# First stage of a long-convolution kernel: 128-row loads of x and v, and a transposed pos_emb in place of transposes on TensorE

## The chip, the cores and the metric

The kernel runs on one core of a Trainium2 chip. The core has TensorE (PE in the profile; its weight loads are PEld), VectorE (DVE), ScalarE (ACT), GpSimd (POOL) and SyncE (SP, which here only issues DMAs), an on-chip memory of 128 partitions (SBUF), an accumulation memory for TensorE (PSUM), and 16 DMA engines that move data between SBUF and the device's DRAM. The metric is the device time of one execution in microseconds. Arrangement of the inputs on the host, before the launch, is not part of it.

## The reference

The inputs x and v are 4 x 12800 x 128 (batch, sequence, channels), pos_emb is 12800 x 64. A filter is made by a small MLP from pos_emb, the product x*v is convolved with it along the sequence, the result is gated with x, and a short gated convolution with two dense layers follows. All is float32; the three weights of the last part come in as float64.

```
h_mlp = np.maximum(pos_emb @ w1, 0.0) @ w2
h_filt = h_mlp * np.exp(-0.01 * pos)[:, None]
u = x * v
y = irfft(rfft(u, n=2 * S) * rfft(h_filt, n=2 * S), n=2 * S)[:, :S]
z = x * y
...
gate_pre[t] += conv_w[k] * z[t + k - 4]      # k = 0..4
out = (sigmoid(gate_pre) * (z @ w_val)) @ w_out
```

## The kernel before

The sequence of 12800 is seen as J x N1 x N2 = 2 x 100 x 64, and the transform is done in two steps, over the 100 and over the 64. The program has three stages, one after the other, with DRAM buffers between them.

**Stage 1** (pools `p1` and `ps1`) is the one that the change touches. Its main loop, `for n in range(N2)`, makes 64 turns, one for each value of the n2 index (`n_seq` pairs n2 with its mirror). A turn does this:

- `fetch` (L323) issues the load of the x and v rows of a later turn, seven ahead, into one of five buffers `ld` (`held`, `XB = 5`). A buffer is 128 partitions x 2048 floats: 1024 of x and 1024 of v. The rows are two batch halves x 50 folded n1 values = 100 rows of 8 KB; they lie in partitions 14 to 113 (`P0 = 14`, `PT = 114`), so that the first half ends, and the second begins, at partition 64.
- `product` (L328) multiplies x by v on VectorE, `mirrored` (L334), once for two turns, makes sum and difference of a pair on VectorE, and GpSimd subtracts one half from the other (L342).
- `spectra` (L346) multiplies by the table `fold`, 12 matmuls of 64 x 512 into two PSUM tiles `fp`; ScalarE copies each into a tile `st` (four of them).
- `store` (L359) writes the 100 rows of `st`, also partitions 14 to 113, to the DRAM buffer `a_u`.

The loads, the stores and the pos_emb loads are issued by SyncE in the order of the code, through a helper `_Split` (L112) that cuts a transfer of 100 rows into one of 96 and one of 4. The scheduler's order is taken from the code (`tc.manual_schedule`). A DMA completes on one of eight semaphores that all DMAs of SyncE and ScalarE take in turn, and an issue waits until the semaphore's previous DMA, eight earlier, has landed.

Between these turns the generator `filt` (L249) computes the filter's first transform in portions. Its parts in order are: 16 steps on pos_emb (TensorE transposes four 100 x 128 blocks into `tp`, VectorE copies `tp` to `posT`, TensorE multiplies by `w1bd` into `gp`, VectorE applies the maximum and the window and writes `g_sb`), then 32 steps `ap` (matmuls with `fwd`, copied by ScalarE to `ag`), then 25 steps on `fk` (tables built by ScalarE and VectorE, then matmuls and a ScalarE copy). Each portion yields a weight, and turn n runs portions until their sum reaches `n_fil * (n + 1) / 58` (L395): the same weight in every turn, about 1.86 of 107.9.

At the start, GpSimd clears partitions 0 to 13 of the five `ld` buffers (L368), VectorE partitions 96 to 127 of two `eo` tiles (L371), and ScalarE issues the loads of 14 constants before its first copy.

**Stage 2** reads `a_u` back in tiles of 128 partitions (`load_pair`, L219), multiplies the spectra and transforms back; **stage 3** makes the last transform, the gates and the output. Neither is changed. Stage 2 cannot begin before the last store of stage 1 has landed.

Of the kernel before, what the change touches and what calls it, by code (L numbers as in the profile page):

```python
# [9 lines left out]
F32 = mybir.dt.float32  # L10
# [3 lines left out]
ALU = mybir.AluOpType  # L14
# [9 lines left out]
B, S, D, FO, KC = 4, 12800, 128, 64, 5  # L24
J, N1, N2 = 2, 100, 64
M = N1 * N2
KG = 8
NF, NH = N1 // 2, 64
P0 = NH - NF
PT = P0 + N1  # L30
R = 4
WARM = 4
NC1 = N1 // 2 + 1
# [2 lines left out]
def _tables():  # L36
    n1, n2 = np.arange(N1), np.arange(N2)
    k1, k2 = np.arange(N1), np.arange(N2)
    th = 2 * np.pi * (np.outer(n1, 4 * k1 + 1) % (4 * N1)) / (4 * N1)
    fwd = np.stack([np.cos(th), np.sin(th), -np.cos(th)], 1)  # L40

    off = 2 * np.pi * (np.outer(2 * n1[:NF] + 1, 4 * k1 + 1) % (8 * N1)) / (8 * N1)
    fold = np.zeros((128, 3, 128))
    for r in (P0, NH):
        fold[r:r + NF, 0, P0:P0 + N1] = np.cos(off) + np.sin(off)
        fold[r:r + NF, 1, P0:P0 + N1] = np.cos(off) - np.sin(off)
    fold[:, 2] = 2 * fold[:, 0].astype(np.float32)

    inv = np.zeros((N1, 2, N2))
    inv[:, 0, :NC1] = (np.cos(th.T) + np.sin(th.T))[:, :NC1] / (2 * M)  # L50
    inv[:, 1, :NC1] = (np.cos(th.T) - np.sin(th.T))[:, :NC1] / (2 * M)
    ph = (np.outer(4 * k1 + 1, n2)[:, :, None] + 4 * N1 * np.outer(n2, k2)[None]) % (4 * M)
    ph = 2 * np.pi * ph / (4 * M)
    wr, wi = np.cos(ph), np.sin(ph)
    f = np.concatenate([np.concatenate([wr, wi], 2), np.concatenate([-wi, wr], 2)], 1)
    g = np.transpose(f, (0, 2, 1))

    ph = (2 * n2[:N2 // 2] + 1 - N2)[:, None] * (4 * N1 * k2 + (4 * k1 + 1)[:, None])[:, None] % (8 * M)
    ph = 2 * np.pi * ph / (8 * M)
    f = np.stack([np.cos(ph), np.sin(ph), -np.cos(ph), np.sin(ph)], 1).reshape(N1, 2, 2, N2 // 2, N2)  # L60
    f = f.transpose(0, 1, 3, 2, 4).reshape(N1 // 2, 2, 2 * N2, N2)
    g = np.concatenate([g[:, :, :N2] + g[:, :, N2:], g[:, :, :N2] - g[:, :, N2:]], 2)


    f = f.transpose(2, 0, 1, 3).reshape(2 * N2, N1 // 2, 1, 2 * N2)
    g = g.reshape(N1 // 2, 2, 2, N2, 2 * N2).transpose(1, 3, 0, 2, 4).reshape(2 * N2, N1 // 2, 2, 2 * N2)
    w = np.concatenate([f, g], 2)
    be = 2 * np.pi * (np.outer(2 * n2 + N2 - 1, k2) % (2 * N2)) / (2 * N2) + np.pi / 4
    cb, sb = np.sqrt(0.5) * np.cos(be), np.sqrt(0.5) * np.sin(be)
    dft = np.stack([np.block([[cb, sb], [-sb, cb]]), np.block([[-sb, cb], [-cb, -sb]])], 1)  # L70
    al = 2 * np.pi * np.outer(2 * n2 - 1, 4 * k1 + 1) / (8 * M)
    tw = np.tile(np.stack([np.cos(al), np.sin(al)], 1), (2, 1, 1))
    win = np.exp(-0.01 * np.arange(S, dtype=np.float32)).reshape(J, N1, N2)
    win = np.transpose(win, (1, 0, 2))
    tabs = {"fwd": fwd, "fold": fold, "inv": inv, "w": w, "dft": dft, "tw": tw, "win": win, "ident": np.eye(128)}
    return {k: np.ascontiguousarray(a, dtype=np.float32) for k, a in tabs.items()}
# [47 lines left out]
def tile_longconv_gate(  # L124
# [107 lines left out]
        return a2, weights[-1][:, p % PG]  # L232

    with tc.tile_pool(name="p1", bufs=1) as p1, tc.tile_pool(name="ps1", bufs=1, space=PSUM) as ps1:
        pos_v = pos.rearrange("(j a n) f -> j a n f", j=J, a=N1)

        g_sb = p1.tile([N1, J, FO, N2], F32, name="g_sb")

        HC, GN, E, XB = 8, 8, 4, 5
        held = [load() for _ in range(XB + 1)]  # L240
        pos_held = held.pop().rearrange("p (i e) -> p i e", i=2)

        def load_pos(c0):
            pos_sb = pos_held[:N1, c0 // HC % 2].rearrange("a (j n f) -> a j n f", j=J, f=FO)
            for j in range(J):
                sync_s.dma_start(out=pos_sb[:, j], in_=pos_v[j][:, c0:c0 + HC])
            return pos_sb

        def filt():  # L249

            parts, pos_sb, after = [], load_pos(0), None
            for c0 in range(0, N2, HC):
                nxt = load_pos(c0 + HC) if c0 + HC < N2 else None
                for j in range(J):
                    for n in range(0, HC, GN):
                        if after:
                            after()
                        tp = ps1.tile([128, 4, N1], F32, name="tp", bufs=1)
                        for q in range(4):
                            nc.tensor.transpose(  # L260
                                out=tp[:, q], in_=pos_sb[:, j, n + 2 * q:n + 2 * q + 2].rearrange("a n f -> a (n f)"),
                                identity=ident[:N1, :N1])
                        posT = p1.tile([128, 4, N1], F32, name="posT", bufs=2)
                        nc.vector.tensor_copy(out=posT, in_=tp)

                        def after(j=j, n0=c0 + n, posT=posT):
                            gp = ps1.tile([N1, GN, FO], F32, name="gp", bufs=1)
                            for q in range(4):
                                nc.tensor.matmul(  # L269
                                    out=gp[:, 2 * q:2 * q + 2].rearrange("a n e -> a (n e)"),  # L270
                                    lhsT=posT[:, q], rhs=w1bd, start=True, stop=True)
                            nc.vector.scalar_tensor_tensor(
                                g_sb[:, j, :, n0:n0 + GN], gp.rearrange("a n e -> a e n"), 0.0,
                                win[:, j, n0:n0 + GN].unsqueeze(1).to_broadcast([N1, FO, GN]),
                                op0=ALU.max, op1=ALU.mult)
                        yield 1.3
                pos_sb = nxt
            after()
            yield 0.7

            for j in range(J):
                for e0 in range(0, FO, E):
# [13 lines left out]
            for k0 in range(0, N1, 4):  # L296
# [9 lines left out]
                    after()  # L306

                def after(k0=k0, fk=fk):
                    gz = ps1.tile([128, 4, 2 * N2], F32, name="gp", bufs=1)
                    for i in range(4):  # L310
                        nc.tensor.matmul(
                            out=gz[:, i], lhsT=ag[:, k0 + i].rearrange("p j e -> p (j e)"), rhs=fk[:, i],
                            start=True, stop=True)
                    nc.scalar.copy(out=ag[:, k0:k0 + 4].rearrange("p k j e -> p k (j e)"), in_=gz)
# [7 lines left out]

        def fetch(i):  # L323
            t = held[i % XB]
            sync_s.dma_start(out=t[P0:PT], in_=xv[n_seq[i]].rearrange("h q w j l b d -> (h q) (w j l b d)"))
            fetched[i] = t.rearrange("p (w e) -> p w e", w=2)

        def product(i):  # L328
            t = fetched.pop(i)
            u = p1.tile([128, J * 2 * XE], F32, name="u", bufs=1) if i % 2 == 0 else t[:, 0]  # L330
            nc.vector.tensor_tensor(u[:PT], t[:PT, 0], t[:PT, 1], op=ALU.mult)
            us[i] = u

        def mirrored(q):  # L334

            a, b = us.pop(2 * q), us.pop(2 * q + 1)
            eo = held_e[q % 2]
            eng = nc.vector if q == N2 // 2 - 1 else nc.gpsimd
            for s, op in ((0, ALU.add), (1, ALU.subtract)):
                nc.vector.tensor_tensor(  # L340
                    eo[:PT, s].rearrange("p j l e -> p (j l e)"), a[:PT], b[:PT], op=op)
                eng.tensor_tensor(  # L342
                    eo[:PT, s, :, 0], eo[:PT, s, :, 0], eo[:PT, s, :, 1], op=ALU.subtract)
            eos[q] = eo

        def spectra(q, s):  # L346
# [13 lines left out]
        def store(q, s, st):  # L360
            sync_s.dma_start(
                out=a_u[:, s, q].rearrange("k e j b d -> k (e j b d)"),
                in_=st[P0:PT].rearrange("k e j b d -> k (e j b d)"))

        fetched, us, eos, last = {}, {}, {}, None
        with tc.manual_schedule():
            for t in held:
                nc.gpsimd.memset(t[0:P0], 0.0)  # L368
            held_e = [p1.tile([128, 2, J, 2, XE], F32, name=f"eo{i}") for i in range(2)]
            for t in held_e:  # L370
                nc.vector.memset(t[96:128], 0.0)  # L371
            fetch(0)
            raw_val, raw_out = _raw(nc, p1, w_val, "raw_val"), _raw(nc, p1, w_out, "raw_out")
            raw_cw = _raw(nc, p1, conv_w.rearrange("k d -> d k"), "raw_cw")
            fil = filt()
            n_fil, spent = 16 * 1.3 + 0.7 + 16 * 0.9 + 16 * 1.5 + 25 * 1.9 + 0.5, 0.0
            for i in range(1, XB):
                fetch(i)
            product(0)
            product(1)  # L380
            mirrored(0)
# [364 lines left out]
                        fill_halo(j, g // EG)  # L746


_INS = ["pos_emb", "w1", "w2", "moe_w_val", "moe_conv_w", "moe_w_out"]

_OUTS = [((J, D, N2, B, N1), "float32")]
_ORDER = np.concatenate([np.arange(NC1), np.arange(N1 - 1, NC1 - 1, -1)])
# [36 lines left out]
```

## Time and profile before

| what | us |
|---|---|
| median of three runs | 1186.93 |
| lowest and highest | 1176.95, 1187.07 |
| the profiled execution's own time | 1178.38 |
| its span, first to last instruction | 1176.2 |
| first matmul of stage 2 in it | 374.6 |

The profile is of one execution. A row of a window view gives a stretch of the span, then for each engine its busy time and instruction count, then the granted TensorE clock, the mean busy share of the 16 DMA engines and the bytes per time that they moved. A row of the chain of waits gives a start, a duration and what the end of the program was waiting for then. A row of a group gives the line, the engine, the operation, its tiles and shapes, the count, the busy time and the mean duration, and then the engine's idle time before these instructions and what ended it.

### The profile page before, as it was taken

To read this page: it belongs to the slowest core of one execution; us is meant where nothing else is said; L and a number is where in the kernel's file an instruction comes from. 1 tells how busy PE (TensorE), PEld (TensorE's weight loads), DVE (VectorE), ACT (ScalarE), POOL (GpSimd) and SP (SyncE) were. 2 spreads that over 40 slices of the span, in tenths; PEclk is the share of its full clock that TensorE was granted. 3 is DMA by queue.
4 is the path that set the end of the run, shared out by engine and by line. 5 is a ranking of instruction groups with operands and counts; after the bars stand their busy time and mean duration, and the time that the engine had idled before them with its cause. 6 is when DMAs were issued, how large, how long until landed. Compare 5 with 4: busy or idle time off the path is not lost.

```text
span 1176.2 us, 17865 instructions
## 1 busy us (share of the span) xinstructions
PE 1052.8 (90%) x6272; PEld 497.3 (42%) x6272; DVE 988.8 (84%) x1168; ACT 617.9 (53%) x1000; POOL 780.4 (66%) x398
## 2 busy tenths in 40 slices
PE   1698999788883999999999999978999999999986
PEld 0355565444431344444444444433444444444432
DVE  4376864798971899999999999818999999999996
ACT  0234766666652243444444443336676767676764
POOL 5123433233320888889988888828889898898880
PEclk9798999999996799999999999989999999999999
DMA  9799999999997688888888999567999999999932
GB/s 216 216 298 350 367 332 312 315 311 312 310 298 265 234 302 302 309 298 302 299 302 293 360 337 327 191 190 217 279 286 282 271 289 278 282 287 279 291 119 111
DMA packets 90968, 329.92 MB, mean 280 GB/s; under 512 B 10094, under 2 KB 17690, under 8 KB 77482
## 3 DMA queue, kind: packets, MB, share of 16 engines
q1 hardware_dynamic: 56904, 249.06, 68.8%
q10 hardware_dynamic: 33978, 79.74, 17.8%
q8 instruction: 51, 0.84, 0.3%
q14 instruction: 35, 0.29, 0.1%
HBM read 197.69 MB, written 131.07 MB: 280 GB/s over the span
## 4 chain that ended last, share of the span: by engine, by line
PE 64%; DMA 22%; ACT 5%; DVE 5%; issue 2%; ACTq 0%; SPq 0%; DVEq 0%
PE c_ps L459 21%; DMA a_u<-st 17%; PE z_ps L443 9%; PE sd L620 9%; PE o_ps L681 6%; PE fp L355 6%; PE v_ps L671 5%; PE tp L634 4%; PE c_ps L428 2%; DVE gt L662 2%; PE ap L289 1%; ACT gt L659 1%; PE gp L269 1%; DMA c_y<-c_sb 1%; ACT o_sb L689 1%
## 5 line engine op out<-in xcount | busy, mean ns | idle before, releaser
L647 POOL TENSOR_TENSOR ext<-yr,xr 128x400 f32<-128x400 f32 x120 | 302.9, 2526 | 41.2 <-DVE yr L645 39.1
L342 POOL TENSOR_TENSOR eo<-eo 114x512 f32<-114x512 f32 x62 | 112.1, 1822 | 219.9 <-DVE eo L340 219.9
L662 DVE SCALAR_TENSOR_TENSOR gt<-ext,cw,gt 128x1600 f32<-128x1600 f32 x128 | 240.7, 1880 | 0.8 <-ACT gt L659 0.8
L355 PE MATMUL fp<-eo,fold 64*128 64x512 f32 x768 | 193.8, 640 | 40.6 <-ACT st L357 23.1
L466 ACT COPY c_sb<-c_ps 128x1024 f32<-128x1024 f32 x100 | 101.3, 1013 | 204.6 <-PE c_ps L459 197.9
L357 ACT COPY st<-fp 128x1024 f32<-128x1024 f32 x128 | 125.2, 1014 | 125.7 <-PE fp L355 63.1
L459 PE MATMUL c_ps<-va,ld 64*128 64x512 f32 (+1 forms) x800 | 166.6, 556 | 0.2 <-ACT c_sb L466 0.2
L449 DVE TENSOR_TENSOR va<-z_ps,h_sb 128x2048 f32<-128x2048 f32 x50 | 114.3, 2285 | 38.2 <-PE z_ps L443 38.2
L528 POOL TENSOR_TENSOR va<-va,vb 128x1024 f32<-128x1024 f32 x50 | 118.4, 2367 | 40.0 <-DVE vb L449 40.0
L443 PE MATMUL z_ps<-ld 64*64 64x512 f32 x800 | 122.5, 621 | 17.6 <-DMA ld<-a_u 15.7
L681 PE MATMUL o_ps<-gd,wout 128*128 128x400 f32 x256 | 112.4, 521 | 19.7 <-DVE gd L676 10.9
L620 PE MATMUL sd<-ag,inv 100*64 100x512 f32 x512 | 128.3, 618 | 1.0 <-ACT sd_sb L627 1.0
L355 PEld LDWEIGHTS fp<-eo,fold 64*128 64x128 f32 x768 | 73.6, 197 | 120.2 <-issue 67.6
L459 PEld LDWEIGHTS c_ps<-va,ld 64*128 64x128 f32 x800 | 74.2, 189 | 113.7 <-issue 110.2
L530 POOL TENSOR_TENSOR va<-va,vb 128x1024 f32<-128x1024 f32 x50 | 118.2, 2363 | 0.0
L627 ACT COPY sd_sb<-sd 128x512 f32<-128x512 f32 x128 | 76.1, 595 | 77.0 <-PE sd L620 54.6
L449 DVE TENSOR_TENSOR vb<-z_ps,h_sb 128x2048 f32<-128x2048 f32 x50 | 114.0, 2279 | 0.0
L671 PE MATMUL v_ps<-ext,wval 128*128 128x400 f32 x256 | 107.1, 500 | 0.0
L340 DVE TENSOR_TENSOR eo<-u,ld 114x1024 f32<-114x1024 f32 x64 | 82.0, 1311 | 20.3 <-PE fp L355 17.5
L459 PE MATMUL c_ps<-vc,ld 64*128 64x512 f32 x400 | 94.2, 589 | 0.0
L634 PEld LDWEIGHTS tp<-ident,sd_sb 128*128 128x128 f32 x512 | 59.4, 143 | 78.9 <-PE sd L620 47.9
L529 POOL TENSOR_TENSOR vc<-vc,vd 128x768 f32<-128x768 f32 x50 | 91.1, 1822 | 1.9
(89 smaller groups left out, 1503.1 us busy)
## 6 DMA issues: line engine op xcount, KB each, us to landing
c_y<-c_sb ACTq DMA_DIRECT2D x100, 512.0 KB
ld<-a_u SPq DMA_DIRECT2D x49, 1024.0 KB
ld<-in_xv_dram SPq DMA_DIRECT2D x64, 768.0 KB
a_u<-st SPq DMA_DIRECT2D x64, 768.0 KB
ag<-c_y SPq DMA_DIRECT2D x116, 384.0 KB
out_dram<-o_sb ACTq DMA_DIRECT2D x32, 800.0 KB
xr<-in_xt_dram SPq DMA_DIRECT2D x31, 800.0 KB
ld<-in_tab_w_dram SPq DMA_DIRECT2D x12, 768.0 KB
```

The costliest lines, as they stand in the source:

```text
L355: nc.tensor.matmul(out=fp[:, h], lhsT=fold[r, w], rhs=eo[r, o, :, l], start=i == 0, stop=i == len(terms) - 1)
L357: nc.scalar.copy(out=st[:, o].rearrange("k j (h b) d -> k h j (b d)", h=2), in_=fp)
L443: nc.tensor.matmul(out=zs[c][half[h]], lhsT=wk[half[c], 0, half[h]], rhs=a2[half[c], h, j], start=True, stop=True)
L449: nc.vector.tensor_tensor(out, z.rearrange("p (b d) -> p b d", d=D).unsqueeze(1).to_broadcast([128, n, B, D]), h_sb.unsqueeze(2).to_broadc ...
L459: nc.tensor.matmul(out=c_ps[:, h, 0:n], lhsT=wk[half[h], 1 + c], rhs=vt[half[h]].rearrange("p b d -> p (b d)"), start=(i == 0), stop=(i == ...
L528: nc.gpsimd.tensor_tensor(va[:, 0:2], va[:, 0:2], vb[:, 0:2], op=ALU.add)
L530: nc.gpsimd.tensor_tensor(va[:, 2:4], va[:, 2:4], vb[:, 2:4], op=ALU.add)
L620: nc.tensor.matmul(out=sd[c * N2:(c + 1) * N2], lhsT=inv[:, c], rhs=ct[c][:, r * B * D:(r + 1) * B * D], start=True, stop=True)
L647: nc.gpsimd.tensor_tensor(e[:, r0 + r], yr, xr, op=ALU.mult)
L662: nc.vector.scalar_tensor_tensor(gt, rows(t, k), cw[:, k:k + 1], gt, op0=ALU.mult, op1=ALU.add)
L671: nc.tensor.matmul(out=v_ps, lhsT=wval, rhs=rows(t)[:, r * ROW:(r + 1) * ROW], start=True, stop=True)
L681: nc.tensor.matmul(out=o_ps, lhsT=wout, rhs=gd, start=True, stop=True)
```

## The change

1. **x and v.** The host appends 14 rows of zeros to each batch half, so `xv` has 128 rows per n2. `fetch` loads all of them with one DMA of 128 x 8 KB (1 MiB, before 800 KB in two DMAs). The rows now begin at partitions 0 and 64. The clears L368 and L371 are gone, and products and differences run over 128 partitions in place of 114.
2. **The table `fold`** has its rows and its result columns moved to begin at 0, so the result's rows lie in partitions 0 to 99 of `st`, and the store reads those. It is still split in 96 and 4.
3. **pos_emb.** The host lays it out as 16 blocks of 128 x 400, transposed. `load_pos` loads one block with one DMA straight into a form that the matmul takes. The transposes, `tp`, `posT` and the copies are gone, and `gp` has two buffers. Five blocks have room; four are loaded between the first loads of x and v, and each of the 16 steps issues one later load at its end.
4. **Weights.** A pos_emb step now counts 1.0 (before 1.3, and 0.7 for the last), so `n_fil` falls from 107.9 to 102.4.

```diff
-    for r in (P0, NH):
-        fold[r:r + NF, 0, P0:P0 + N1] = np.cos(off) + np.sin(off)
+    for r in (0, NH):
+        fold[r:r + NF, 0, :N1] = np.cos(off) + np.sin(off)
...
-        pos_held = held.pop().rearrange("p (i e) -> p i e", i=2)
...
+        PE1 = GN // 2 * N1
+        pos_held = held.pop()[:, 0:2048 // PE1 * PE1].rearrange("p (i q a) -> p i q a", q=GN // 2, a=N1)
+        parts, pos_ts = [(c0, j) for c0 in range(0, N2, GN) for j in range(J)], []
+
+        def load_pos():
+            if len(pos_ts) < len(parts):
+                c0, j = parts[len(pos_ts)]
+                t = pos_held[:, len(pos_ts) % (2048 // PE1)]
+                nc.sync.dma_start(out=t.rearrange("p q a -> p (q a)"), in_=pos[j, c0 // GN])
+                pos_ts.append(t)
...
-                        for q in range(4):
-                            nc.tensor.transpose(
-                                out=tp[:, q], in_=pos_sb[:, j, n + 2 * q:n + 2 * q + 2].rearrange("a n f -> a (n f)"),
-                                identity=ident[:N1, :N1])
-                        posT = p1.tile([128, 4, N1], F32, name="posT", bufs=2)
-                        nc.vector.tensor_copy(out=posT, in_=tp)
...
+            for i, (n0, j) in enumerate(parts):
+                gp = ps1.tile([N1, GN, FO], F32, name="gp", bufs=2)
+                for q in range(GN // 2):
+                    nc.tensor.matmul(
+                        out=gp[:, 2 * q:2 * q + 2].rearrange("a n e -> a (n e)"),
+                        lhsT=pos_ts[i][:, q], rhs=w1bd, start=True, stop=True)
...
+                load_pos()
+                yield 1.0
...
-            sync_s.dma_start(out=t[P0:PT], in_=xv[n_seq[i]].rearrange("h q w j l b d -> (h q) (w j l b d)"))
+            nc.sync.dma_start(out=t, in_=xv[n_seq[i]].rearrange("h q w j l b d -> (h q) (w j l b d)"))
...
-                in_=st[P0:PT].rearrange("k e j b d -> k (e j b d)"))
+                in_=st[:N1].rearrange("k e j b d -> k (e j b d)"))
...
-            for t in held:
-                nc.gpsimd.memset(t[0:P0], 0.0)
...
-            for t in held_e:
-                nc.vector.memset(t[96:128], 0.0)
...
             for i in range(1, XB):
                 fetch(i)
+                load_pos()
...
+    xv = np.stack(pairs, 3)
+    xv = np.concatenate([xv, np.zeros_like(xv[:, :, :NH - NF])], 2)
+    pos = np.asarray(inputs["pos_emb"]).reshape(J, N1, N2 // KG, KG // 2, 2, FO)
+    pos = np.transpose(pos, (0, 2, 4, 5, 3, 1)).reshape(J, N2 // KG, 2 * FO, KG // 2 * N1)
```

SyncE's queue after the first loads, before the change (`ld_102` to `ld_106` are the five x and v buffers, `ld_107` holds pos_emb, and each row is one DMA with its partitions x elements):

```order
L120 DMA ld_104<-in_xv_dram 96x2048
L120 DMA ld_104<-in_xv_dram 4x2048
L120 DMA ld_107<-in_pos_emb_dram 96x512
L120 DMA ld_107<-in_pos_emb_dram 4x512
...
L120 DMA ld_105<-in_xv_dram 96x2048
L120 DMA ld_105<-in_xv_dram 4x2048
...
L120 DMA a_u_60<-st_155 96x2048
L120 DMA a_u_60<-st_155 4x2048
```

The same queue from its first row, with the change:

```order
L306 DMA ld_102<-in_xv_dram 128x2048
L306 DMA ld_103<-in_xv_dram 128x2048
L245 DMA ld_107<-in_pos_dram 128x400
L306 DMA ld_104<-in_xv_dram 128x2048
...
L245 DMA ld_107<-in_pos_dram 128x400 x2
L306 DMA ld_105<-in_xv_dram 128x2048
L245 DMA ld_107<-in_pos_dram 128x400 x2
L118 DMA a_u_60<-st_144 96x2048
L118 DMA a_u_60<-st_144 4x2048
```

The first pos_emb load was the 17th DMA of this queue, behind eight x and v loads; it is now the third, behind two. A turn without pos_emb issues three DMAs here where it issued four.

TensorE's order from the first turn on, before (`fp` is the spectrum of x*v, `tp` the transpose, `gp` the pos_emb product):

```order
L355 MATMUL fp_156<-eo0_115,fold_63 128x512 x4
L355 MATMUL fp_162<-eo0_115,fold_63 128x512 x2
L260 MATMUL tp_174<-ident_68,ld_107 128x100 x4
L269 MATMUL gp_181<-w1bd_69,posT_179 100x128 x4
L260 MATMUL tp_187<-ident_68,ld_107 128x100 x4
L355 MATMUL fp_199<-eo0_115,fold_63 128x512 x2
L355 MATMUL fp_203<-eo0_115,fold_63 128x512 x4
```

And with the change:

```order
L334 MATMUL fp_145<-eo0_110,fold_63 128x512 x4
L334 MATMUL fp_151<-eo0_110,fold_63 128x512 x2
L252 MATMUL gp_155<-w1bd_69,ld_107 100x128 x4
L252 MATMUL gp_162<-w1bd_69,ld_107 100x128 x4
L334 MATMUL fp_173<-eo0_110,fold_63 128x512 x2
L334 MATMUL fp_177<-eo0_110,fold_63 128x512 x4
```

A `gp` matmul stood behind a transpose and VectorE's copy of it; it now reads the loaded tile itself, and two steps stand in a row between the first two turns.

More of the change, by code (lines that the diff above doesn't have):

```diff
@@ L28 @@
 NF, NH = N1 // 2, 64
-P0 = NH - NF
-PT = P0 + N1
 R = 4
@@ L43, in _tables @@
     fold = np.zeros((128, 3, 128))
-    for r in (P0, NH):
-        fold[r:r + NF, 0, P0:P0 + N1] = np.cos(off) + np.sin(off)
-        fold[r:r + NF, 1, P0:P0 + N1] = np.cos(off) - np.sin(off)
+    for r in (0, NH):
+        fold[r:r + NF, 0, :N1] = np.cos(off) + np.sin(off)
+        fold[r:r + NF, 1, :N1] = np.cos(off) - np.sin(off)
     fold[:, 2] = 2 * fold[:, 0].astype(np.float32)
@@ L234, in tile_longconv_gate @@
     with tc.tile_pool(name="p1", bufs=1) as p1, tc.tile_pool(name="ps1", bufs=1, space=PSUM) as ps1:
-        pos_v = pos.rearrange("(j a n) f -> j a n f", j=J, a=N1)
         g_sb = p1.tile([N1, J, FO, N2], F32, name="g_sb")
-        HC, GN, E, XB = 8, 8, 4, 5
+        GN, E, XB = 8, 4, 5
         held = [load() for _ in range(XB + 1)]
-        pos_held = held.pop().rearrange("p (i e) -> p i e", i=2)
[L243 to L247, printed above, removed]
@@ L249, in filt @@
-        def filt():
[L251 to L258, printed above, removed]
-                        for q in range(4):
-                            nc.tensor.transpose(
-                                out=tp[:, q], in_=pos_sb[:, j, n + 2 * q:n + 2 * q + 2].rearrange("a n f -> a (n f)"),
-                                identity=ident[:N1, :N1])
-                        posT = p1.tile([128, 4, N1], F32, name="posT", bufs=2)
[L264 to L279, printed above, removed]
@@ new lines, in filt @@
+        def filt():
+            for i, (n0, j) in enumerate(parts):
[4 more added lines that the diff above has]
+                        lhsT=pos_ts[i][:, q], rhs=w1bd, start=True, stop=True)
+                nc.vector.scalar_tensor_tensor(
+                    g_sb[:, j, :, n0:n0 + GN], gp.rearrange("a n e -> a e n"), 0.0,
+                    win[:, j, n0:n0 + GN].unsqueeze(1).to_broadcast([N1, FO, GN]),
+                    op0=ALU.max, op1=ALU.mult)
+                load_pos()
+                yield 1.0
@@ L308, in after @@
                 def after(k0=k0, fk=fk):
-                    gz = ps1.tile([128, 4, 2 * N2], F32, name="gp", bufs=1)
+                    gz = ps1.tile([128, 4, 2 * N2], F32, name="gp", bufs=2)
                     for i in range(4):
@@ L330, in product @@
             u = p1.tile([128, J * 2 * XE], F32, name="u", bufs=1) if i % 2 == 0 else t[:, 0]
-            nc.vector.tensor_tensor(u[:PT], t[:PT, 0], t[:PT, 1], op=ALU.mult)
+            nc.vector.tensor_tensor(u, t[:, 0], t[:, 1], op=ALU.mult)
             us[i] = u
@@ L339, in mirrored @@
             for s, op in ((0, ALU.add), (1, ALU.subtract)):
[L340 to L343, printed above, removed]
+                nc.vector.tensor_tensor(eo[:, s].rearrange("p j l e -> p (j l e)"), a, b, op=op)
+                eng.tensor_tensor(eo[:, s, :, 0], eo[:, s, :, 0], eo[:, s, :, 1], op=ALU.subtract)
             eos[q] = eo
@@ L375, in tile_longconv_gate @@
             fil = filt()
-            n_fil, spent = 16 * 1.3 + 0.7 + 16 * 0.9 + 16 * 1.5 + 25 * 1.9 + 0.5, 0.0
+            n_fil, spent = 16 * 1.0 + 16 * 0.9 + 16 * 1.5 + 25 * 1.9 + 0.5, 0.0
             for i in range(1, XB):
                 fetch(i)
+                load_pos()
             product(0)
@@ L746, in tile_longconv_gate @@
                         fill_halo(j, g // EG)
-_INS = ["pos_emb", "w1", "w2", "moe_w_val", "moe_conv_w", "moe_w_out"]
+_INS = ["w1", "w2", "moe_w_val", "moe_conv_w", "moe_w_out"]
 _OUTS = [((J, D, N2, B, N1), "float32")]
@@ L771 @@
         pairs.append(np.transpose(a, (5, 0, 4, 2, 3, 1, 6)))
-    feeds[:0] = [("xv", np.stack(pairs, 3)), ("xt", xt)]
+    xv = np.stack(pairs, 3)
+    xv = np.concatenate([xv, np.zeros_like(xv[:, :, :NH - NF])], 2)
+    pos = np.asarray(inputs["pos_emb"]).reshape(J, N1, N2 // KG, KG // 2, 2, FO)
+    pos = np.transpose(pos, (0, 2, 4, 5, 3, 1)).reshape(J, N2 // KG, 2 * FO, KG // 2 * N1)
+    feeds[:0] = [("xv", xv), ("xt", xt), ("pos", pos)]
     for name, a in feeds:
```

## The prediction

> **What bounds the kernel now.** I read the slices of the page first, to find the stage's limit; then the chain of waits; then windows, to price transfers of different shape; then groups and timeline, for what leaves.
>
> ```profile
> span 1176.2 us, 17865 instructions
> PE   1698999788883999999999999978999999999986
> DMA  9799999999997688888888999567999999999932
> GB/s 216 216 298 350 367 332 312 315 311 312 310 298 265 234 302 302 309 298 302 299 302 293 360 337 327 191 190 217 279 286 282 271 289 278 282 287 279 291 119 111
> ```
>
> A slice is 29.4 us. Over the first twelve, which are stage 1, the DMA engines are the full resource (9), TensorE mostly is not (8). And full is not the same as fast: the first two slices are full at 216 GB/s, the fifth at 367. The chain of waits says the same in order of time:
>
> ```profile
> 7.93 9.16 DMA w1bd<-in_w_dram
> 17.12 8.89 DMA ident<-in_tab_ident_dram
> 26.03 9.13 DMA raw_out<-in_moe_w_out_dram
> 35.18 3.83 DMA ld<-in_pos_emb_dram
> 39.01 0.91 PE tp L260 x4
> ...
> 87.11 8.32 DMA ld<-in_pos_emb_dram
> ...
> 159.85 10.61 DMA a_u<-st
> 170.52 10.50 DMA a_u<-st
> ...
> 371.90 2.60 DMA ld<-a_u
> ...
> 374.63 2.11 PE z_ps L443 x8
> ```
>
> To 39 us the chain is loads that wait for loads; from 160 us on it is one store after another, a step of 10.6 us for two turns; stage 2 starts at 374.6. So stage 1 ends when the DMA engines have done their work. What that work costs depends on the shape of the transfer:
>
> ```profile
> 0.00:372.00 372.00, 285.46 (x1960) 156.30 (x1960) 249.35 (x305) 193.17 (x286) 121.04 (x71) 0.93 0.94 299
> 30.00:60.00 30.00, 18.90 (x97) 11.75 (x98) 10.99 (x14) 9.06 (x9) 3.33 (x2) 0.72 0.79 216
> 8.00:30.00 22.00, 5.49 (x12) 1.86 (x12) 9.71 (x8) 0.00 (x0) 9.27 (x5) 0.92 1.00 224
> 120.00:160.00 40.00, 40.00 (x432) 23.65 (x428) 30.08 (x19) 29.99 (x34) 15.86 (x9) 1.00 1.00 359
> 160.00:330.00 170.00, 144.53 (x948) 78.09 (x946) 135.47 (x201) 113.27 (x198) 56.52 (x33) 0.98 0.97 313
> 340.00:344.00 4.00, 3.50 (x10) 1.57 (x12) 2.61 (x3) 1.64 (x3) 1.42 (x1) 0.57 0.99 328
> 376.00:386.00 10.00, 8.40 (x60) 3.35 (x56) 9.18 (x6) 1.14 (x3) 4.55 (x3) 0.67 1.03 406
> ```
>
> The last two numbers of a row are DMA share and GB/s. At 8 to 30 us there are x and v loads of 100 rows and small constants, no store: full at 224. At 376 to 386 us, in stage 2, there are loads of 128 partitions alone: full at 406. At 340 to 344 there are stores of 100 rows alone: 328. The mixtures lie between, 359 and 313. What was in flight shows in the issues of these stretches:
>
> ```profile
> 331.48 0.69 SPq L120 DMA_DIRECT2D ld<-in_xv_dram  x2
> 333.36 16.46 SPq L120 DMA_DIRECT2D a_u<-st  x12
> ld<-in_xv_dram SPq DMA_DIRECT2D x64, 768.0 KB
> ld<-in_xv_dram SPq DMA_DIRECT2D x64, 32.0 KB
> ld<-a_u SPq DMA_DIRECT2D x2, 1024.0 KB
> ```
>
> The last x and v load was issued at 331.5, then only stores. The third and fourth rows are all of stage 1's x and v loads, the last is what the stretch 376 to 386 moved.
>
> **The change, part by part.** The sum is DMA time against the profiled execution: 1178.38 us for a span of 1176.2, so 2.2 lie outside; it is 8.6 below the median of the runs shown and near their lowest.
>
> *DMA work before.* Share 0.94 of 372 us is 350 busy, 22 idle. The loads are 64 x 800 KB = 52.4 MB and the stores as much; pos_emb is 3.3 MB; 299 GB/s x 372 us is 111.2 MB in all, so 3.0 MB are constants and stage 2's first tiles. For the stores I have two ends: 328 GB/s (alone) and 400 (as well as 128 partitions); I take 350, near the one that was measured on stores and below the 359 of the full mixture: 52.4/0.35 = 150 us. pos_emb ran where the rate was 216 to 350, about 12 us; the 3.0 MB at 216, about 14. The loads are left with 350 - 150 - 12 - 14 = 174 us, 301 GB/s: above their rate alone, below the mixture, as it must be.
>
> *Loads of 128 rows.* 64 x 1 MiB = 67.1 MB, 14.7 MB more. The rate lies between 224 (nothing gained) and 406 (the 128-partition row). I take 400, since the row nearest in shape, 1 MiB into 128 partitions, has it: 168 us, 6 less than before. So 28% more bytes cost about nothing, if the rate holds. Break-even for this term alone is 67.1/0.174 = 386 GB/s, close by; this is the term on which the sign hangs.
>
> *Stores.* Same bytes; the rows move from partitions 14-113 to 0-99. No row shows that; ends: 400 GB/s (131 us) and 224 (234 us). I take 150, unchanged.
>
> *pos_emb.* The same 3.3 MB, in 16 DMAs for 32; with 128 rows at 350 to 400 it is 9 us, 3 less. Rest 14. Sum 168 + 150 + 9 + 14 = 341, 9 less than before.
>
> *Idle DMA time.* The stretch 30 to 60 us loses 0.21 x 30 = 6.3 us, because SyncE's pos_emb issues stood behind eight loads and behind semaphores that ScalarE's constants held, and then TensorE's order stood behind pos_emb:
>
> ```profile
> 17.48 5.49 PE L355 MATMUL fp<-eo,fold 64*128 64x512 f32 x12 [17.48 <-POOL eo L342]
> 39.01 0.90 PE L260 MATMUL tp<-ident,ld 100*128 100x100 f32 x4 [16.03 <-DMA ld<-in_pos_emb_dram]
> 30.25 0.39 ACTq L81 DMA_DIRECT2D raw_cw<-in_moe_conv_w_dram  x1
> 31.97 1.93 ACT L357 COPY st<-fp 128x1024 f32<-128x1024 f32 x2
> 43.19 4.64 PE L355 MATMUL fp<-eo,fold 64*128 64x512 f32 x12
> ```
>
> Turn 0's matmuls begin at 17.5, turn 1's at 43.2. With pos_emb third in the queue the 16.0 us wait goes. Late next is ScalarE, which cannot copy before its last constant is issued at 30.25; the third generation of each semaphore comes sooner if 128-row loads are faster, so I put turn 1 at about 25. I count 5 of the 6.3 us; the second pos_emb wait (8.3 us at 87) costs the DMA engines nothing, since they were full there. The other idle time, at the start and in the last 40 us, where stage 2's tiles wait for stores, stays: 22 - 5 = 17.
>
> *Sum.* Stage 1 ends at 341 + 17 = 358 in place of 372: -14, and to the same tail **1178.4 - 14 = 1164 us**.
>
> *What lies beside other work.* These leave the engines and are costed at nothing, or nearly:
>
> ```profile
> L260 PE MATMUL tp<-ident,ld 100*128 100x100 f32 x64 | 9.3, 273 | 18.3 <-DMA ld<-in_pos_emb_dram 18.3
> L264 DVE COPY posT<-tp 128x400 f32<-128x400 f32 x16 | 9.1, 566 | 18.0 <-PE tp L260 18.0
> 0.74 8.76 POOL L368 MEMSET ld<- 14x2048 f32 x5 [0.29 <-POOLq L762]
> L371 DVE MEMSET eo<- 32x2048 f32 x2 | 3.5, 1765 | 0.9 <-issue 0.9
> ```
>
> TensorE loses 9.3 of 285 us and VectorE 12.6 of 249, in a stage of 358: not the limit, though at 120 to 160 us TensorE is busy all 40 us, so no turn there gets shorter. The clears lie under the first loads; GpSimd's end at 9.5 us, well before the matmul at 17.5 that follows its first subtraction. Operations over 128 partitions in place of 114 take the time of their row length, which stays; bounds 0 and 128/114, 12%, of VectorE's 249, which would still be under 358. The portions' smaller weight gives each turn 1.77 in place of 1.86 of filter work, within the same 64 turns.
>
> *The added wait.* From the fifth on, a pos_emb load waits for TensorE's step that frees its slot, and behind it in SyncE's queue stand the next store and the next x and v load. Four to five loads are ahead of use, about 25 us at 5 us a turn, and the step is in the turn that TensorE is at; so 0, and at most one turn, 5 us, once. SyncE's other wait gets looser: three issues a turn on eight semaphores, not four, let 2.7 turns be in flight where 2 were.
>
> **Rivals.**
>
> *A. As summed:* 1164, with 1152 to 1174 for its own bounds (stores at 380 or at 328 GB/s, with the new loads at 400: -12 and +10).
>
> *B. Stores get faster too.* If the slow 100-row loads were what delayed the stores between them, these go from 350 to 400 GB/s: 131 us, -19 more, 1145. For it: 359 GB/s at 120 to 160 us, with the same transfers. Against it: 328 with stores alone.
>
> *C. A ceiling on the mixture.* No slice of this stage passes 367. At 359 for everything, 119.5 + 3.3 + 3.0 MB take 350 us, and with 17 idle stage 1 ends at 367: 1173, no change that can be told. Against it: 406 at 376 to 386 us, loads alone. [...]
>
> *D. Stores get slower (the other side).* That 100 rows load at 224 and 128 partitions at 406 says that the spread over partitions matters, by more than 100/128. The stored rows lay 50 below partition 64 and 50 above; now 64 and 36. If the fuller half sets the pace, a store takes 64/50 of 150, 192 us: +42 - 14, 1206. It decides from about 164 us on (320 GB/s for the stores). Against it: the half was not yet shown to be what counts, and a turn has room between stores. [...]
>
> *E. Loads gain nothing.* If they are slow for another reason and stay at 301 GB/s, 67.1 MB take 223 us, +49 for -6: 1219. Against it: the 406 row.
>
> **How the numbers follow.** About 1% (12 us) is what a measurement can tell from no change. Chances: A 0.50, B 0.15, C 0.14, D 0.13, E 0.08. The likeliest is A, 1164. The range 1140 to 1192 holds A, B and C and the beginning of D; D's and E's ends, 2 in 10, are left out. Faster by over 1% (below 1166.6) are B and somewhat over two thirds of A, and a little of C: 0.53. Same: the rest of A, most of C, a little of D: 0.29. Slower: most of D, and E: 0.18.
>
> **What would show it.** Loads right: early stretches without stores at 350 to 400 GB/s. Start right: turn 1's matmuls near 25 us, no wait for pos_emb. Stores: a stretch of stores alone at 328 to 350, and steps of about 10 us for two turns in the chain; at 12, D. End: stage 2's first matmul near 360. The forecast is wrong if the loads stay under 350 GB/s, if stores fall under 320, or if TensorE, not DMA, carries the chain from 160 us on.

## The result, and the profile after

| | before | after |
|---|---|---|
| median | 1181.94 us | 1164.05 us |
| lowest and highest, four runs each | 1173.24, 1187.07 | 1161.68, 1167.67 |
| the profiled execution's own time | 1178.38 | 1167.67 |
| its first matmul of stage 2 | 374.6 | 362.5 |

The ratio of after to before is 0.9853, with a 95% interval of 0.9818 to 0.9888: 1.5% faster, 18 us by the medians. The profiled execution of after is the slowest of its four, so the two traces differ by 10.7 us only. Three executions of before beside the experiments (1258.5, 1741.4 and 2095.7 us) ran far slower than all others and are left out here. In the traces stage 1 ends 12.1 us earlier; what follows it takes 803.0 us, before 801.6.

The span and the slices of the changed kernel's page, each slice 29.1 us:

```profile
span 1165.5 us, 17562 instructions
PE   4899887887764999999999999979999999999986
DMA  9999999999987588988888998558999999999932
GB/s 364 350 417 403 361 352 345 353 341 350 344 268 286 209 311 300 317 300 302 303 312 287 362 339 321 178 176 218 283 288 285 264 292 278 278 289 284 284 119 113
```

The first two slices, 216 GB/s before, are 364 and 350 now, and the third passes 400. From the fifth on the rate is back at 341 to 361, with the same transfers. Windows of the changed kernel (the last two numbers are DMA share and GB/s) say it by stretches:

```profile
0.00:362.00 362.00, 277.69 (x1896) 150.30 (x1896) 228.67 (x287) 192.07 (x291) 117.02 (x66) 0.95 0.96 349
8.00:30.00 22.00, 13.68 (x68) 7.34 (x68) 14.91 (x14) 5.77 (x6) 9.14 (x4) 1.00 1.04 394
60.00:120.00 60.00, 56.59 (x562) 33.56 (x562) 38.15 (x30) 38.97 (x45) 29.82 (x14) 1.00 1.01 409
120.00:160.00 40.00, 34.93 (x380) 20.48 (x376) 19.09 (x16) 20.28 (x24) 11.74 (x8) 1.00 0.99 350
160.00:330.00 170.00, 135.20 (x684) 69.33 (x680) 132.29 (x202) 105.35 (x193) 54.98 (x32) 0.94 0.97 348
```

Loads and constants at 8 to 30 us now run at 394 (224 before), loads and stores together at 60 to 120 us at 409. From 160 us on it is 348, with the DMA engines as full as before. The timeline of the changed kernel shows the start of turns 0 and 1 and of stage 2:

```profile
14.20 4.43 PE L334 MATMUL fp<-eo,fold 64*128 64x512 f32 x12 [14.20 <-POOL eo L322]
19.90 0.39 ACTq L79 DMA_DIRECT2D raw_cw<-in_moe_conv_w_dram  x1
22.68 2.90 PE L334 MATMUL fp<-eo,fold 64*128 64x512 f32 x12 [2.13 <-ACT st L336]
362.46 3.54 PE L419 MATMUL z_ps<-ld 64*64 64x512 f32 x16 [16.29 <-DMA ld<-a_u]
```

Turn 1 starts at 22.7 us, not 43.2, and waits for ScalarE's copy, which waits behind its last constant (19.9; before 30.25). Not all of this lead lasts. The starts of the turns (first `fp` matmul, us), with those of three of the experiments below:

| turn | 1 | 20 | 40 | 57 | 63 | stage 2 |
|---|---|---|---|---|---|---|
| before | 43.2 | 143.4 | 239.8 | 329.1 | 353.8 | 374.6 |
| after | 22.7 | 118.5 | 225.6 | 316.6 | 341.0 | 362.5 |
| `e4_store112` | 22.8 | 115.8 | 209.7 | 299.6 | 318.1 | 339.9 |
| `e12_piece4` | 22.8 | 133.6 | 232.9 | 320.9 | 349.7 | 372.7 |
| `e2_pos` | 28.5 | 134.7 | 239.9 | | 354.9 | 375.4 |

The lead of after is 25 us at turn 20 and 12.5 at turn 57: turns 20 to 57 take 5.35 us each, before 5.02. What they wait for is in the chain of waits of the changed kernel (start, duration, what for) and in SyncE's own waits at 160 to 330 us (total, times, longest):

```profile
148.71 16.37 DMA a_u<-st
165.58 15.20 DMA a_u<-st
...
239.59 16.71 DMA a_u<-st
256.81 14.93 DMA a_u<-st
```

```profile
SPq L118 <- DMA ld<-in_xv_dram: 75.1, 31, 3.5
SPq L306 <- DMA a_u<-st: 47.1, 29, 2.1
```

The chain is stores still, a step of some 16 us for three turns. SyncE, which issues everything here, stands 122 of 170 us before a semaphore of a DMA that has not landed. L118 is the helper `_Split`, which cuts a store into 96 and 4 rows; L306 is `fetch`.

### The profile page after: what moved, and what is told of

It reads as the page before. It is cut to its first block, busy times and chain, and to the rows that moved or that the text cites. A ratio compares the mean times of both kernels' runs of the same rounds, so it can differ in the third digit from the quotient of the medians.

```text
span 1165.5 us, 17562 instructions
## 1 busy us (share of the span) xinstructions
PE 1046.1 (90%) x6208; PEld 492.1 (42%) x6208; DVE 969.3 (83%) x1150; ACT 615.7 (53%) x1000; POOL 775.2 (67%) x393
## 4 chain that ended last, share of the span: by engine, by line
PE 58%; DMA 28%; ACT 6%; DVE 4%; issue 2%; SPq 1%; ACTq 0%; DVEq 0%
PE c_ps L435 21%; DMA a_u<-st 19%; PE sd L596 9%; PE z_ps L419 9%; DMA ld<-in_xv_dram 6%; PE o_ps L657 6%; PE v_ps L647 5%; PE tp L610 5%; PE c_ps L404 2%; DVE gt L638 2%; PE fp L334 2%; ACT gt L635 1%; ACT o_sb L665 1%; DMA c_y<-c_sb 1%; ACT sg L642 1%
## 5 line engine op out<-in xcount | busy, mean ns | idle before, releaser
L322 POOL TENSOR_TENSOR eo<-eo 128x512 f32<-128x512 f32 x62 | 116.8, 1904 | 212.0 <-DVE eo L321 212.0
L610 PE MATMUL tp<-ident,sd_sb 128*128 128x128 f32 x512 | 81.9, 286 | 5.4 <-ACT sd_sb L603 3.8
```

What stands on the lines that cost most here:

```text
L610: nc.tensor.transpose(out=tp[:, b], in_=t[:, b], identity=ident)
```

## The experiments

The question after this result: the expected time was met, but which of the sum's terms were right, and why are the late turns slower than before's? The first two experiments do one part of the change each. The others take the changed kernel and change the store or the load. None leaves out any computation; where 112 rows are stored, the 12 beyond the result are zeros. The medians of before, measured anew beside each group of runs, lie between 1181.2 and 1183.9, so 3 us between kernels of different groups say nothing.

| label | stored rows, by partition | median us | ratio to before, 95% | stage 2 at |
|---|---|---|---|---|
| (after) | 0-95, 96-99 | 1164.05 | 0.9853 [0.9818, 0.9888] | 362.5 |
| `e1_rows128` | as after | 1168.36 | 0.9876 [0.9839, 0.9914] | 364.2 |
| `e2_pos` | as before | 1177.56 | 0.9833 [0.9770, 0.9895] | 375.4 |
| `e3_store14` | 14-109, 110-113 | 1154.62 | 0.9749 [0.9662, 0.9835] | 350.6 |
| `e4_store112` | 0-111 in one | 1139.99 | 0.9647 [0.9599, 0.9694] | 339.9 |
| `e5_store96_16` | 0-95, 96-111 | 1151.06 | 0.9732 [0.9678, 0.9785] | 347.0 |
| `e6_store2` | 2-97, 98-101 | 1159.32 | 0.9809 [0.9771, 0.9847] | 354.3 |
| `e7_store12` | 12-107, 108-111 | 1163.37 | 0.9837 [0.9796, 0.9878] | 358.9 |
| `e8_load112` | as after; load 8-119 in one | 1164.25 | 0.9843 [0.9795, 0.9891] | 365.9 |
| `e9_tiny` | 0-111 in one, and 16 x 4 bytes in | 1141.18 | 0.9648 [0.9613, 0.9683] | 340.3 |
| `e10_store112_8` | 8-119 in one | 1136.92 | 0.9627 [0.9595, 0.9659] | 335.4 |
| `e11_spread4` | 0-95, then 96, 100, 104, 108 | 1160.33 | 0.9792 [0.9755, 0.9829] | 360.6 |
| `e12_piece4` | 0-111 in one, and 96-99 again | 1180.77 | 0.9987 [0.9949, 1.0026] | 372.7 |

Of the ten runs of `e2_pos` nine lie between 1170.7 and 1181.8 and one at 1155.0; its printed ratio rests on the two lowest, so its median is used here, 6 us below the 1183.1 of before beside it.

### One part of the change alone

`e1_rows128` is before with items 1 and 2 of the change, pos_emb as it was:

```
-            sync_s.dma_start(out=t[P0:PT], in_=xv[n_seq[i]]...)
+            nc.sync.dma_start(out=t, in_=xv[n_seq[i]]...)
-                in_=st[P0:PT]...
+                in_=st[:N1]...
```

> The kernel before with the x and v part of the change alone: one load of 128 rows per n2, no clears, stores from partitions 0 to 99; pos_emb is loaded, transposed and queued as before. Theory (the gain is DMA time of the loads): from 8 to 30 us the DMA engines move 340 to 400 GB/s in place of 224, and stage 2 starts 8 to 16 us earlier, so 1162 to 1171 us beside a before of about 1178; the wait for pos_emb before turn 1 stays, at 30 to 39 us. Rival (the gain is the start, by pos_emb): within 4 us of before.

`e2_pos` is before with items 3 and 4, x and v as they were:

```
-                        tp = ps1.tile([128, 4, N1], F32, name="tp", bufs=1)
...
-                        nc.vector.tensor_copy(out=posT, in_=tp)
+                        lhsT=pos_ts[i][:, q], rhs=w1bd, start=True, stop=True)
+                load_pos()
```

> The kernel before with the pos_emb part alone: 16 transposed blocks, no transposes, weights as in the change; x and v loads stay at 100 rows in two DMAs, clears and stores as before. Theory: the first wait goes (turn 1 near 30 us in place of 43), but the DMA engines were full and moved only 224 GB/s, so what is gained at the start is given back by about 160 us: 0 to -6 us against before. Rival (the gain is the start): -10 to -16 us.

Windows of `e1_rows128`, then of `e2_pos`:

```profile
8.00:30.00 22.00, 5.30 (x16) 2.36 (x16) 10.32 (x7) 3.21 (x3) 7.77 (x4) 0.80 1.01 363
160.00:330.00 170.00, 142.20 (x840) 74.11 (x836) 135.86 (x205) 111.40 (x200) 56.55 (x34) 0.96 0.99 362
```

```profile
8.00:30.00 22.00, 8.08 (x32) 4.42 (x34) 11.41 (x10) 3.21 (x3) 7.87 (x5) 0.97 0.95 203
160.00:330.00 170.00, 135.79 (x790) 70.75 (x786) 127.07 (x197) 105.77 (x191) 51.66 (x30) 0.97 0.96 308
```

Items 1 and 2 carry the gain: 1168.36 is 14.8 below the 1183.1 of before, and the early rate goes to 363. Turn 1 still waits for pos_emb, but starts at 33.5. The pos_emb part alone leaves the rates at 203 and 308, as before. It wins 15 us at turn 1 (28.5 for 43.2), and by turn 40 nothing of that is left: the DMA engines had the same bytes at the same rate. Beside the new loads it is worth about 4 us (1168.36 to 1164.05), which is not clear of the noise: the two intervals overlap.

### Where the stored rows lie

`e3_store14` is the changed kernel with the result at partitions 14 to 113, as before:

```
-        fold[r:r + NF, 0, :N1] = np.cos(off) + np.sin(off)
+        fold[r:r + NF, 0, P0:P0 + N1] = np.cos(off) + np.sin(off)
-                in_=st[:N1]...
+                in_=st[P0:PT]...
```

> The changed kernel with the stored rows put back to partitions 14 to 113; all else as changed. Theory (the place of the stored rows does not count; late in stage 1 the turns are slow for another reason): within 4 us of the changed kernel, 1160 to 1168, and 340 to 356 GB/s from 160 to 330 us. Rival (the fuller lower half of the partitions, 64 to 36, slows the stores): 8 to 25 us faster than the changed kernel, 1140 to 1156.

1154.62, in the range of the rival and some 9 us below after, though the two intervals still overlap by a hair (0.9835 and 0.9818). The gain is not where it was looked for: 160 to 330 us run at 348 GB/s as in after, but 105 to 160 us at 400 against 360. `e6_store2` and `e7_store12` are the same edit with `P0` 2 and 12.

> The changed kernel with the stored rows at partitions 2 to 101 (62 below partition 64, 38 above), in 96 and 4 rows; the piece of 4 rows is then at partitions 98 to 101, over the border of a group of four. Theory 1 (the piece of 4 rows from one group of four partitions is what is slow): as with the rows at 14 to 113, stage 2 starts at 348 to 354 us, 1150 to 1158 us. Theory 3 (the fuller lower half, 62 to 38, slows the stores): as the changed kernel, 359 to 364 us, 1160 to 1168.

> The changed kernel with the stored rows at partitions 12 to 111 (52 below partition 64, 48 above), in 96 and 4 rows; the piece of 4 rows is then at partitions 108 to 111, one whole group of four. Theory 1: as the changed kernel, stage 2 starts at 359 to 364 us, 1160 to 1168 us. Theory 3: as with the rows at 14 to 113, 348 to 354 us, 1150 to 1158.

`e7_store12` stores 52 rows below partition 64 and 48 above, nearly the even split of before, and gains nothing (1163.37); `e6_store2`, 1159.32, fits neither of its ranges. So the split between the halves is not what counts. What remained was the group of four partitions in which the small piece lies: one group in after and in `e7_store12`, two in `e3_store14` and `e6_store2`. `e11_spread4` puts its rows in four groups:

```
+    kc = np.r_[0:96, 96:112:4]
...
+            for k, r in ((slice(0, 96), slice(0, 96)), (slice(96, N1), slice(96, 112, 4))):
```

> The changed kernel, with the store still as 96 rows and 4 rows, but the 4 rows now lie at partitions 96, 100, 104 and 108, each in another group of four partitions. Theory 'group of four': the small piece is slow because all its rows come out of one group of four partitions; spread over four groups it costs little, and the time is 1137 to 1148 us, with the second stage starting at 338 to 348 us. Rival 'small piece': a transfer of 4 rows beside one of 96 is slow wherever its rows lie; then the time is as the changed kernel's, 1158 to 1168 us, with the second stage at 357 to 365 us.

1160.33: inside what the rival expected, and far from the 1137 to 1148 of the group. That theory falls. Over five places the time went from 1154.6 to 1164.1, in no order that a rule explains. What puts `e3_store14` at the lower end stays open.

### How the store is cut

`e4_store112` stores 112 rows, 12 of them zeros, in one transfer instead of 96 and 4 (`a_u` has 112 rows then, 6.3 MB more in the stage). `e5_store96_16` stores the same 112 as 96 and 16. The edit of the first:

```
+NS = 112
...
-            sync_s.dma_start(
+            nc.sync.dma_start(
-                in_=st[:N1]...
+                in_=st[:NS]...
```

> The changed kernel with the store made one DMA of 112 rows (12 of them zeros, into a buffer padded to 112 rows) in place of 96 and 4 rows; the result is the same. It moves 12% more bytes per store, but a turn issues two DMAs in place of three, so that eight in flight are four turns. Theory (late in stage 1 SyncE waits for the DMA eight earlier, and the DMA engines run dry): a turn from 160 to 330 us falls from 5.36 to 4.7 to 5.0 us, stage 2 starts 12 to 25 us earlier, 1139 to 1152 us. Rival 1 (the mixture of loads and stores has a ceiling near 350 GB/s): 5.6 us a turn, 8 to 16 us slower than the changed kernel. Rival 2 (four st tiles set the pace): within 5 us of the changed kernel.

> The changed kernel with the store in two DMAs, of 96 and of 16 rows (12 of them zeros, buffer padded to 112 rows): three DMAs a turn on SyncE as in the changed kernel, but every DMA engine gets the same number of rows and the second piece is spread over partitions 96 to 111. Theory 1 (what is slow late in stage 1 is the piece of 4 rows, which only four DMA engines move, all from partitions 96 to 99): as with the store of 112 rows, stage 2 starts at 338 to 346 us, 1138 to 1148 us. Theory 2 (three issues a turn with eight DMAs in flight): as the changed kernel, 356 to 364 us, 1158 to 1168.

Windows of `e4_store112`, then SyncE's waits in it at 160 to 330 us, then pieces of its chain:

```profile
60.00:105.00 45.00, 43.66 (x420) 25.06 (x419) 32.12 (x26) 29.65 (x36) 21.93 (x10) 1.00 1.01 421
105.00:160.00 55.00, 53.11 (x572) 31.85 (x570) 29.35 (x24) 33.45 (x38) 24.77 (x12) 1.00 1.01 423
160.00:330.00 170.00, 140.86 (x708) 70.19 (x705) 131.21 (x204) 111.18 (x197) 52.54 (x30) 0.92 0.99 391
```

```profile
SPq L307 <- DVE eo L322: 45.2, 12, 4.8
SPq L307 <- DVE u L313: 25.0, 8, 6.0
SPq L307 <- DVE fk L285: 21.0, 5, 6.9
```

```profile
163.48 16.72 DMA a_u<-st
187.05 16.63 DMA a_u<-st
232.11 5.07 PE fp L335 x12
262.73 5.12 PE fp L335 x12
```

With 12% more bytes to store, stage 1 ends 22.6 us earlier and the kernel is 24 us faster than after. 423 GB/s of loads and stores together also settles that no ceiling near 359 held the mixture. From some 200 us on SyncE waits for VectorE instead of DMAs, and the chain has TensorE's matmuls: the stage comes near the point where DMA no longer sets its end. `e5_store96_16` lies between its two expectations (1151.06, 385 GB/s at 160 to 330 us): the same bytes in two transfers cost 11 us more than in one.

Two things change when the second transfer goes: a turn issues two DMAs, not three, on the eight semaphores, and the four rows no longer travel apart. `e9_tiny` brings back only the first: behind the store of 112 rows comes a transfer of 64 bytes.

```
+            mark = p1.tile([16, 1], F32, name="mark", bufs=8)
+            nc.sync.dma_start(out=mark, in_=t_ident[0:16, 0:1])
```

> The changed kernel with the store made one DMA of 112 rows, and behind each store one more DMA of 64 bytes (16 partitions x 4 bytes of a table, into a scratch tile that nothing reads): three DMAs a turn on SyncE again, with no bytes to speak of. Theory 2 (part of what the store of 112 rows gained is that eight DMAs in flight are four turns): slower than without the small DMA by 6 to 14 us, 1146 to 1154, as with the store of 96 and 16 rows, with SyncE's waits for the DMA eight earlier back. Theory 1 alone (all of it came from the piece of 4 rows): 1137 to 1143 us, as without it.

A window of `e9_tiny` and SyncE's waits in it at 160 to 330 us:

```profile
160.00:330.00 170.00, 142.45 (x716) 71.27 (x712) 131.94 (x204) 112.05 (x199) 52.57 (x30) 0.92 0.99 393
```

```profile
SPq L307 <- DMA a_u<-st: 39.1, 24, 2.5
SPq L345 <- DMA ld<-in_xv_dram: 20.1, 22, 1.5
```

SyncE's waits for unlanded DMAs are back, 59 us of them, and the time is that of `e4_store112` (1141.18). A count of three on the semaphores does not cost it by itself. So the reason given for `e4_store112`, fewer transfers in flight, falls, though its time came out. `e12_piece4` then brings back four full rows in place of the 64 bytes, written to a scratch tensor:

```
+            nc.sync.dma_start(
+                out=a_p[:, s, q]..., in_=st[96:100]...)
```

> The kernel with one store transfer of 112 rows a turn (e4_store112), and behind each a second transfer that writes rows 96 to 99 once more to a scratch tensor that nothing reads: 4 rows, 128 KB, 3% more bytes in the stage. Theory 'small piece': the full-length rows that only a few DMA engines move are what costs, whatever goes with them; the time goes back to 1154 to 1170 us, the second stage starts at 354 to 364 us, and the stretch from 160 to 330 us moves 340 to 360 GB/s. Rival '96 rows': it is the transfer of 96 rows that is slower than one of 112; then this kernel pays only for its bytes, 4 to 6 us, which is 1141 to 1148 us with the second stage at 342 to 348 us.

Its sizes are wrong in that text: four rows are 32 KB, 2.1 MB in 64 turns, 1.7% of the stage's 126 MB; the 4 to 6 us for them are right, since 2.1 MB at 420 GB/s is 5. Windows of `e12_piece4`:

```profile
60.00:105.00 45.00, 35.81 (x312) 20.02 (x310) 23.48 (x19) 22.98 (x28) 13.69 (x8) 0.96 1.00 367
160.00:330.00 170.00, 138.43 (x788) 71.07 (x784) 136.20 (x206) 109.49 (x197) 56.32 (x33) 0.97 1.00 388
```

The time is 1180.77, above the range of either theory. 39.6 us come with the four rows in place of the 64 bytes: by an estimate at 420 GB/s 5 for their bytes, and some 35 for the rest. The two runs differ in more than the number of rows: the 64 bytes are a load, the four rows a store, which also keeps the tile `st` busy until it lands (ScalarE's copy waited for that once in stage 1, 3.8 us). And the expectation was wrong as to where: the loss is at 60 to 160 us (turn 20 starts 18 us later than in `e4_store112`) and at the end, while 160 to 330 us run at 388 GB/s, nearly the 393 of `e9_tiny`. So this run does not repeat the slow late turns of after.

From after to `e4_store112` 24 us are gained in spite of 6.3 MB more. These bytes are at most 15 us at 420 GB/s, an estimate, since DMA does not set the whole end of `e4_store112`; so the piece would be worth 24 to 39 us there, and from `e3_store14` 15 to 30 by the same sum. That 35 and 39 lie close is no proof of one mechanism, as the two kernels lose the time in different stretches.

The traces settle more of it, since they record when each share of a transfer lands. A transfer of 96, 112 or 128 rows, and that of 64 bytes, lands in 16 shares, a piece of four rows in four (besides one event at its issue). For the loads of x and v issued in a stretch, the median time from the eighth share to the last, in us:

| | 30 to 60 us | 60 to 105 | 105 to 160 | 160 to 330 |
|---|---|---|---|---|
| after | 2.4 | 4.5 | 7.5 | 7.7 |
| `e3_store14` | 1.4 | 3.5 | 5.7 | 6.9 |
| `e12_piece4` | 3.7 | 8.1 | 6.4 | 6.3 |
| `e5_store96_16` | 2.2 | 2.1 | 5.1 | 4.7 |
| `e9_tiny` | 1.8 | 2.5 | 3.0 | 4.1 |
| `e4_store112` | 1.8 | 2.0 | 2.7 | 3.6 |
| `e10_store112_8` | 2.2 | 2.0 | 2.5 | 2.0 |

In after some shares fall behind between 60 and 160 us, by more than a turn, and stay there. They are those of the piece: in all 11 turns at 105 to 160 us, and in 23 of 33 at 160 to 330, its four shares land some 0.31 us, the time of one packet of 8 KB, after the last four shares of the 96 rows ahead of it. So the 409 GB/s belong to the stretch in which these shares are still falling behind, and the slow late turns, with SyncE waiting for whole transfers, to the one in which they are late. The DMA share does not show it (0.97 in after, 0.99 in `e4_store112`). In `e12_piece4` a share is late too, but in none of the 57 turns from 30 to 330 us is it one that the piece follows, so its loss is not the same thing.

Last, the place once more, with no small piece: `e10_store112_8` has 112 rows at partitions 8 to 119, 56 in each half, where `e4_store112` has 64 and 48:

```
-                in_=st[:NS]...
+                in_=st[P0 - K0:P0 - K0 + NS]...
```

> The changed kernel with the store made one DMA of 112 rows from partitions 8 to 119 (the stored rows at 14 to 113, the rest zeros), in place of 0 to 111. Theory (with no piece of 4 rows the place does not count): within 4 us of the 112 rows from partition 0, 1136 to 1144. Rival (rows more evenly above and below partition 64 are faster by themselves, as 14 to 113 seemed against 0 to 99): 5 to 12 us faster, 1128 to 1135.

1136.92 beside 1139.99: the place makes 3 us at most, no more than the noise between groups. It is the fastest kernel of the study, 27 us below after (ratio to before 0.9627, 0.9595 to 0.9659).

### Which part of the load's change counts

`e8_load112` loads 112 rows at partitions 8 to 119 in one transfer:

```
-            nc.sync.dma_start(out=t, in_=xv[n_seq[i]]...)
+            nc.sync.dma_start(
+                out=t[L0:L1], in_=xv[n_seq[i]]...[L0:L1])
```

> The changed kernel with the x and v load cut to 112 rows, partitions 8 to 119, in one DMA: 12.5% fewer bytes than 128 rows, still one DMA and still all 16 engines (7 rows each, not 8). Theory (128 rows are fast because each DMA engine then writes its own partitions): from 8 to 30 us only 220 to 320 GB/s, stage 2 starts 5 to 20 us later than with 128 rows, 1166 to 1185 us. Rival (they are fast because one DMA replaces two, and the piece of 4 rows is gone from the loads): 360 to 400 GB/s from 8 to 30 us, and 0 to 8 us faster than with 128 rows.

Its first window, for the 394 of after:

```profile
8.00:30.00 22.00, 6.35 (x30) 3.61 (x32) 12.66 (x11) 2.54 (x3) 9.41 (x5) 0.92 1.04 255
```

Loads of 112 rows are slow alone, 255 GB/s, as the theory expected, and yet the kernel takes 1164.25, below its range and as after does with 128: the 8.4 MB that it saves are 20 us at 420 GB/s. So the step from 112 to all 128 gives the high early rate and pays for it in bytes. What both share against before is the single transfer, with no 4-row piece behind it, besides the place of the stored rows and the pos_emb part; no run leaves the load's piece out alone. The reason that the theory gives, which engine writes which partitions, was a guess of the author: the trace does not number the engines, so no run shows it.

## Why the prediction was right, point by point

**The bound: right.** DMA share 0.96 over stage 1, TensorE 278 of 362 us, the chain from 160 us on stores. VectorE's sums and differences took 1240 ns each over 128 partitions, before 1311 over 114; GpSimd's took 1904 for 1822.

**Loads at 400 GB/s: right alone, mis-sized in the mixture.** 394 was measured where only loads run. The sum carried that rate through the stage: 119.5 MB in 168 + 150 us is 376 GB/s for loads and stores together. Measured were 409 at 60 to 120 us and 348 at 160 to 330. The errors nearly cancel: 0.96 x 362 is 348 us of DMA work, where the sum had 341. `e8_load112` shows the weak step of the argument: a rate measured alone does not say what the transfer costs among others.

**Stores at 150 us: not shown wrong, but for a wrong reason.** "Same bytes" was the argument, and the moved rows the risk. Moving them cost at most the 9 us between `e3_store14` and after. A larger cost lay in a thing that the change left alone, the cut into 96 and 4 rows: storing 112 rows at once gained 24 us, and the sum held that inside "350 GB/s". One sign could not be read: after the last load no stretch had stores alone and full engines (share 0.67 to 0.85 and 219 to 238 GB/s at 332 to 344 us). The other, the step in the chain, was 10.7 us for two turns, nearer the 10 of the forecast than the 12 of D.

**pos_emb, -3 and -5: about right.** Together -8 were forecast; the runs give 4 beside the new loads (`e1_rows128` to after, within the noise) and 6 alone, with `e2_pos` showing how the start is given back. Idle DMA time is 0.04 x 362 = 14 us, forecast 17.

**The start: right.** Turn 1 at 22.7 (forecast about 25), behind ScalarE's constants as said, with no wait for pos_emb.

**The end: right.** Stage 2 at 362.5, forecast near 360; 1164.05 us, forecast 1164. That the times agree to a tenth is luck: -14 were forecast from one execution of 1178.4, the medians differ by 18 and the two traces by 10.7, and the loads' and stores' errors nearly cancel.

**Rival B**, faster stores, did not happen in after. **Rival C**, a ceiling at 359, falls with 409 GB/s in after and 423 in `e4_store112`. **Rival D**, the fuller half, for which `e3_store14` alone seemed to speak, falls with `e7_store12` and with `e10_store112_8`: by its arithmetic 64 rows in place of 56 would cost 64/56 of 150 us, 21 us more, and 3 were measured. D argued from rates of loads alone; at 8 to 30 us they were 224 GB/s for 100 rows in two transfers (before), 255 for 112 in one (`e8_load112`) and 394 for 128 in one (after); what makes the last step no run shows. **Rival E** falls with 394 GB/s.

**What stays open.** That the late shares of after are those of the piece is shown, and that stage 1 ends 23 us earlier with one store of 112 rows. How much of that is the piece's own work is not. The typical packet of 8 KB takes 309 ns in the trace, so if the same four DMA engines took one more each turn, and set the pace, it would be 64 x 0.309 = 20 us, an estimate, less than the 24 us that were gained. That the four are the same each turn is an assumption of this estimate: the landings have 16 shares for 96, 112 or 128 rows and four for the piece, but the trace does not number the engines, so no run here shows which they are. It is not known why three shares of a load are late in after and two in `e3_store14`, nor which share is late in `e12_piece4`. Nor is it known whether the piece would cost as much without the waits on the semaphores, since no run had the one without the other.

## What to carry to other kernels

Where DMA sets the time, look at how a transfer is cut before its bytes: storing 12 rows of zeros in one transfer, so that no four rows travelled apart, gained 24 us, and four rows more in a transfer of their own cost 39.6 over one of 64 bytes. A full DMA share says little about this; when the shares of a transfer land says more. Price a transfer in the mixture in which it runs, by a window of that stretch, not by its rate alone. And an earlier start is worth nothing by itself where the bytes that follow set the end: `e2_pos` started turn 1 15 us earlier and ended stage 1 when before did.

## What was not expected of the hardware

- Loads and stores together reached 423 GB/s over 55 us (`e4_store112`), above the 406 of loads alone at 376 to 386 us in before.
- A transfer of 64 bytes behind each store cost 1 us in all, which is within the noise (`e9_tiny`, 1141.18 beside 1139.99); one of 32 KB in four rows cost 39.6 more.
- 112 rows load at 255 GB/s alone, 128 rows at 394: 14% more rows, 55% more rate.
- At 160 to 330 us of after, 13 of a load's 16 shares land within 8.8 us of its issue and the last three at 13.4 to 13.8 us (medians).
